# Long-convolution front of a gated block on one core: two channel halves staggered, one second-stage transform of kv per block, an order written as a table

## The chip, the cores and the metric

One core of a Trainium2 chip runs the whole program. The metric is the device time of one execution in microseconds (us). The kernel before has a median of 561.63 us over three runs (561.54, 561.63, 564.53). The profiled execution took 562.82 us, of which 561.0 us lie between its first and its last instruction (the span); its granted TensorE clock was 0.996 of full speed.

Engine names are those of the profile: PE (matrix multiply), PEld (its weight load), DVE (vector engine), ACT (scalar engine), POOL (GpSimd), SP (the engine that issues most DMAs). All engines take their instructions in the order of the program.

## The reference

S = 2048 rows, D = 448 channels, F = 1792. Cut to what matters:

```python
mod = (silu(c) @ w_mod).reshape(6, D)          # sa, ca, ga, sb, cb, gb
h = layernorm(q) * (1 + ca) + sa
kv = causal_conv4(k, shift_k) * v              # four taps per channel
y = irfft(rfft(pad(kv)) * rfft(pad(ssm_k)))[:S] + kv * ssm_D
x = q + ga * (h * y)                           # first half: the long convolution
h = layernorm(x) * (1 + cb) + sb
x = x + gb * ((sigmoid(h @ w_gate) * (h @ w_up)) @ w_down)
```

Everything is float32. The Fourier transforms are done as matrix products.

## The kernel before, in words

The program has two parts: the convolution (to about 158.8 us, where the first matmul `gu` of the gated unit starts) and the gated unit behind it, which is a long stream of matmuls. The change touches the first part and leaves the instructions of the second as they are, but for three small items named below.

The channels are cut into two halves of C = 224, h = 0 and 1. A transform of 4096 points is done in two stages. In stage one (`stage1`, L193) four matmuls of 64x128x224 go into a PSUM pair, and ACT evicts it into the tile `ak[h]` (kernel spectrum) or `av[h]` (kv); eight such groups fill one tile. (The profile has two records for each float32 matmul, so its counts are twice these.) Then DVE turns each of the 8 blocks of 896 columns (`turn`, L189, a 32x32 transpose). In stage two (`stage2_k`, L278) a block of `ak` is multiplied by `w2` on PE and evicted by ACT in place. For kv (`stage2_v`, L292) the same is done twice for each block: `w2[r, 0]` gives the real and imaginary parts, `w2[r, 1]`, which holds the same numbers rolled by 32, gives them swapped. So each block has 8 matmuls into two PSUM pairs, `pts[0]` and `pts[1]`. DVE multiplies each pair by the kernel's spectrum (L303, two products `m` of 128x896), PE adds up the products with `wa` (L319, tile `sa`, 4 matmuls) and DVE turns `sa` back into `av` (L321). Sixteen blocks (2 halves x 8) go through this loop, one block behind in `stage2_back`. Last, `stage_out` (L330) makes 16 rows of the output `y` out of all eight blocks of a half.

What feeds it: the four taps of the short convolution. `k` comes transposed in the tile `kT`, 112 partitions (a quarter of the channels, `ct`). There are 16 units, four quarters by four groups of rows. In 11 of them a first product is made by ACT (`conv_first`, L221) and three further taps are added by DVE (`conv_tap`, L226: one SCALAR_TENSOR_TENSOR of 112x512, out of `kT` and an accumulator, both in SBUF). In four units ACT makes all four products (L245), and one unit is done on PE with diagonal matrices (L260). PE transposes the sum into the PSUM pair `kv` (L263), and DVE multiplies `v` by it (`conv_mul`, L272).

Order: both halves of the kernel spectrum's stage one come first, then the short convolution of all channels together, then stage one of kv, and then the loop of 16 blocks. In that loop stand, beside the blocks: the remaining turns of `av` and `ak[1]`, stage two of `ak[1]`, the statistics of the layernorm of `q` (`ln1_stats`, L429, ACT), its gates (`gates`, L448; normalising on POOL for h = 0 and on ACT for h = 1, `modulate` L463 on POOL) and the six matrix products of `mod` (`mod_parts`, L369, `mod_sum`, L388). `mod` 3 and 5 come after the loop, between the outputs of the convolution and the first `gu`. The whole is recorded in a hand-written order; PSUM has eight banks in four pairs, two under the name `t`, and one each under `sa` and `y`.

All DMAs of the first part are issued by SP in program order, but two small ones by ACT.

Of the kernel before, what the change touches and what calls it, by code (L numbers as in the profile page):

```python
# [81 lines left out]
def adaln_conv_glu_kernel(ctx: ExitStack, tc: tile.TileContext, q, kT, v, ssm, shift, dskip,  # L82
# [26 lines left out]
    inb = big.tile([P, 16 * C], F32, tag="in", name="inb")  # L109
    taken = []  # L110

    def quad(tag, bufs, name):

        if tag == "in":
            at = len(taken) % 4 * 4 * C
            taken.append(name)
            return inb[:, at:at + 4 * C].rearrange("p (a c) -> p a c", c=C)
        return late["pg" if tag == "G" else "rb"].tile([P, 4, C], F32, tag=tag, bufs=bufs, name=name)

    def whole(t):  # L120
        return t.rearrange("p a c -> p (a c)").rearrange("p (g d) -> p g d", g=2)
# [8 lines left out]
    zc = pz.tile([P, NG, P], F32, name="zc")  # L130
    ktl = pk.tile([DT, 4, NG + 3, P], F32, name="kT")
    xin = {}
    early = big.tile([P, NG + 2, C], F32, tag="a0", name="early")
    ka, kb = slice(0, 11), (slice(11, 15), slice(15, NG + 3))

    def load_ssm(h, i, parts=(slice(0, 4),)):
        if (h, i) not in xin:
            xin[h, i] = early[:, 4 * i:4 * i + 4] if h else quad("in", 4, f"ssm{h}_{i}")
        t = xin[h, i]
        for s in parts:  # L140
            nc.sync.dma_start(t[:, s], ssm[:, h, 4 * i + s.start:4 * i + s.stop])
            if i == 0 and s.start == 0:
                dr = early[0:1, NG + h]
                nc.sync.dma_start(dr, dskip[:, h])
                (POOL if h else DVE).tensor_add(t[0:1, 0], t[0:1, 0], dr)

    def load_v(k):
        xin["v", k] = whole(quad("in", 4, f"v{k}") if k not in (4, 5) else spare[:, (k - 4) * 4 * C:(k - 3) * 4 * C].rearrange("p (a c) -> p a c", c=C))
        nc.sync.dma_start(xin["v", k], v[:, 2 * k:2 * k + 2])

    def load_k(ct, part):
        at = DT * ct * (NG + 3) * P
        w = (part.stop - part.start) * P
        at += DT * P * part.start
        nc.sync.dma_start(ktl[:, ct, part].rearrange("p a b -> p (a b)"), kT[at:at + DT * w].rearrange("(p x) -> p x", p=DT))
# [1194 lines left out]
```

## Time and profile before

| item | value |
| --- | --- |
| median of 3 runs | 561.63 us |
| profiled execution | 562.82 us |
| its span | 561.0 us |
| PE busy in the span | 544.9 us (97%) |
| DVE busy | 435.4 us (78%) |
| ACT busy | 271.9 us (48%) |
| POOL busy | 57.4 us (10%) |
| first turn of `ak[0]` on DVE | 16.04 us |
| first product `m` on DVE | 71.52 us |
| last turn of `sa` on DVE ends | 147.06 us |
| first `gu` on PE | 158.79 us |
| HBM read / written | 63.58 / 28.44 MB |

How to read it: the share of busy time is a mean over two parts with different limits. A row of a group names the line, the engine, the operation and the tiles (out<-in), the shape, how many there are, their busy time together, the mean of one in ns, and how long the engine had been idle in front of them and for whom. The chain is followed back from the last instruction to whatever released each step. A PE that counts as busy is not PE at its peak, since its ends are modelled.

### The profile page before, as it was taken

Reading aid. Unit: us, or ns where it says so; the run is one execution under the profiler, and the core shown is the slowest. Engines: PE = TensorE matmul, PEld = TensorE weight load, DVE = VectorE, ACT = ScalarE, POOL = GpSimd, SP = SyncE. Lnnn points to the kernel's source line nnn. Section 1 sums busy time; section 2 is a strip of 40 time slices with the busy share of each in tenths; the row PEclk is TensorE's granted clock in tenths of the full one; section 3 lists DMA queues with packets and bytes.
Section 4 is the critical chain, followed back from the end, with each engine's and each line's share of the span. In section 5 each row is a group of like instructions: output and inputs, shape, how many; then the busy total and the mean of one; then the engine's idle time right before and its main releaser. Section 6 shows DMA issues by size and latency. Waiting matters only on the chain.

```text
span 561.0 us, 7853 instructions
## 1 busy us (share of the span) xinstructions
PE 544.9 (97%) x3074; PEld 423.5 (75%) x3074; DVE 435.4 (78%) x544; ACT 271.9 (48%) x471; POOL 57.4 (10%) x52
## 2 busy tenths in 40 slices
PE   7898899999999999999999999999999999999997
PEld 6577632333567888888888888888888888888886
DVE  0879789969789887898998888885555556879565
ACT  4977676971477586366546462332122222334120
POOL 1000006979400000000000000000000000000000
PEclk9989999999999999999999999999999999999999
DMA  8993591200530408494968195676464662220103
GB/s 277 281 273 116 169 323 58 76 2 2 149 109 1 160 4 303 148 377 190 350 237 322 76 362 168 227 265 232 137 206 129 205 214 111 77 103 10 56 1 131
DMA packets 24857, 93.06 MB, mean 166 GB/s; under 512 B 3058, under 2 KB 4212, under 8 KB 23796
## 3 DMA queue, kind: packets, MB, share of 16 engines
q1 hardware_dynamic: 18372, 67.66, 38.0%
q10 hardware_dynamic: 6448, 24.90, 11.4%
q8 instruction: 24, 0.39, 0.3%
q14 instruction: 13, 0.11, 0.1%
HBM read 63.58 MB, written 28.44 MB: 164 GB/s over the span
## 4 chain that ended last, share of the span: by engine, by line
PE 76%; DVE 12%; DMA 4%; issue 3%; ACT 3%; SPq 1%; DVEq 0%; ACTq 0%
PE d L911 23%; PE b L877 16%; PE c L877 10%; PE a L877 10%; PE gu L1000 4%; PE s2v L300 3%; DVE m L303 3%; DMA kT<-in_kT_dram 2%; PE y L335 2%; PE sa L319 2%; PE s1v L199 2%; DVE av L321 2%; DMA early<-in_ssm_dram 1%; PE kv L260 1%; DVE av L191 1%
## 5 line engine op out<-in xcount | busy, mean ns | idle before, releaser
L911 PE MATMUL d<-wd,h 128*128 128x448 f32 x666 | 144.4, 366 | 0.6 <-DVE wd L497 0.5
L911 PEld LDWEIGHTS d<-wd,h 128*128 128x128 f32 x666 | 124.7, 188 | 13.5 <-DVE wd L497 1.4
L877 PE MATMUL b<-xt,ring 128*128 128x512 f32 x408 | 99.0, 391 | 0.0
L877 PEld LDWEIGHTS b<-xt,ring 128*128 128x128 f32 x408 | 76.5, 188 | 14.9 <-issue 0.2
L926 DVE TENSOR_TENSOR x<-x,d 128x896 f32<-128x896 f32 x55 | 59.5, 1084 | 16.6 <-PE d L911 16.6
L877 PE MATMUL a<-x,ring 128*128 128x512 f32 x264 | 63.8, 389 | 0.0
L877 PEld LDWEIGHTS a<-x,ring 128*128 128x128 f32 x264 | 49.6, 188 | 10.2
L886 ACT ACTIVATE h<-st 128x512 fp32r<-128x512 f32 x55 | 34.6, 629 | 31.4 <-DVE st L895 19.0
L889 DVE TENSOR_TENSOR h<-st,h 128x512 fp32r<-128x512 f32 x55 | 37.8, 688 | 12.5 <-ACT h L886 12.2
L892 ACT ACTIVATE st<-st 128x512 f32<-128x512 f32 x24 | 15.2, 631 | 63.6 <-DVE st L1237 35.8
L1000 PE MATMUL gu<-x,ring 128*128 128x512 f32 x176 | 42.5, 395 | 0.1
L1191 ACT ACTIVATE st<-st 128x512 f32<-128x512 f32 x12 | 7.6, 631 | 67.8 <-DVE st L1190 67.8
L303 DVE TENSOR_TENSOR m<-s2v,ak 128x896 f32<-128x896 f32 x32 | 33.2, 1078 | 9.2 <-PE s2v L300 8.2
L1000 PEld LDWEIGHTS gu<-x,ring 128*128 128x128 f32 x176 | 32.7, 188 | 7.7 <-ACT full L800 0.6
L877 PE MATMUL c<-x,ring 128*128 128x512 f32 x144 | 34.8, 390 | 0.0
L858 ACT ACTIVATE ring<-sum 128x512 fp32r<-128x512 f32 x28 | 17.3, 626 | 32.2 <-DVE sum L839 16.8
L877 PEld LDWEIGHTS c<-x,ring 128*128 128x128 f32 x144 | 27.0, 188 | 5.2
L300 PE MATMUL s2v<-av,w 64*64 64x448 f32 x256 | 30.8, 546 | 0.1
L877 PE MATMUL c<-xt,ring 128*128 128x512 f32 x120 | 29.2, 389 | 0.0
L319 PE MATMUL sa<-m,wa 128*64 128x448 f32 x128 | 27.4, 552 | 0.0
L877 PEld LDWEIGHTS c<-xt,ring 128*128 128x128 f32 x120 | 22.5, 188 | 4.6
L895 DVE TENSOR_TENSOR st<-st 128x512 f32<-128x512 f32 x24 | 16.6, 690 | 11.9 <-ACT st L892 11.7
(184 smaller groups left out, 787.9 us busy)
## 6 DMA issues: line engine op xcount, KB each, us to landing
fd<-ring ACTq DMA_DIRECT2D x35, 512.0 KB, 5.2
ring<-fd SPq DMA_DIRECT2D x35, 512.0 KB, 3.9
wdk<-wd ACTq DMA_DIRECT2D x7, 896.0 KB, 5.9
wd<-wdk SPq DMA_DIRECT2D x7, 896.0 KB, 4.8
inb<-in_wgu_dram SPq DMA_DIRECT2D x6, 1024.0 KB, 5.3
x<-in_q_dram SPq DMA_DIRECT2D x4, 896.0 KB, 8.5
wm<-in_wmod_dram SPq DMA_DIRECT2D x8, 392.0 KB, 5.5
out_dram<-x SPq DMA_DIRECT2D x7, 448.0 KB, 2.6
```

Source lines behind the costliest of these rows:

```text
L300: PE.matmul(pts[b][c:c + 64, ex, :D], w2[r:r + 64, ex], xs_[b][r:r + 64], start=True, stop=True)
L303: DVE.tensor_mul(m[b], rows(pts[b]), ks[b].unsqueeze(1).to_broadcast([P, 2, D]))
L319: PE.matmul(wide[r, b, :, :56], wa[:, b, r], m[b][:, ex], start=True, stop=True)
L858: ACT.activation(forms[name, i][:, 0], w_src(name), AF.Copy)
L877: PE.matmul(pt, wh(s, t), x[:, k], start=start and m == 0, stop=stop and m == len(ops) - 1, skip_group_check=True)
L886: ACT.activation(hh, h, AF.Copy)
L889: DVE.tensor_sub(hl, h, hh)
L892: ACT.activation(y[:, 0], y[:, 0], AF.Sigmoid)
L895: DVE.tensor_mul(y[:, 0], y[:, 0], y[:, 1])
L911: PE.matmul(y, h[:, (2 * e + i) * P:(2 * e + i + 1) * P], x, start=m == 0, stop=m == len(ops) - 1)
L926: DVE.tensor_add(y, y, rows(pt))
L1000: PE.matmul(pt[:, g], plain(q, t)[:, s, g, f * P:f * P + P], xf[xs_[b]][:, k], start=m == 0, stop=m == 10, skip_group_check=True)
```

## The change

- The order of the whole first part is a table of 436 items (`ORDER`), which `run` plays one by one: `t1.0.2.1.d.0` is tap 1 of half 0, rows 4i to 4i+3 with i = 2, quarter 1 of the half, on DVE, into accumulator 0; `p` is POOL, `a` ACT; `:0` to `:3` is the PSUM pair. The two halves follow each other, half 1 behind half 0.
- kv's stage two is done once for a block (`do_s2v`: 4 matmuls, one PSUM pair). DVE multiplies this pair twice: by the block of `ak` (`do_m0`) and by a copy of that block in which neighbouring groups of 32 partitions are swapped (`do_m1`). The copy is made by four DMAs of 32x896 from SBUF to SBUF (`do_kx`), in three homes in turn. `w2` loses its second half, and the right half of `wa` takes its rows in swapped order.
- The short convolution: the first product of all 16 units (`p`) is made by POOL, three taps of each unit of half 0 and two of half 1 by DVE, one product of each unit of half 1 by ACT. The diagonal matrices are gone. `k` is padded to 128 partitions and loaded in four parts a quarter; `v` and `w_mod` are cut and padded likewise.
- A new map of SBUF: the tiles of the first part are fixed places in a few large ones (`inb`, `av0`, `ak0`, `av1`, `spare`, `kTa`, `kTb`, `m`, `zc`).
- `mod` 3 and 5 move into the loop. `ln1_end`, in before half on ACT, is two DVE operations for each of its four groups.
- The four PSUM pairs have names of their own (`t0`, `t1`, `sa`, `y`).

```diff
+ORDER = """
+kt.0.0.0 kt.0.1.0 ssm.0.2 kt.0.1.1 kt.0.1.2 v.0.3 zc.3 kt.0.0.1 zc.2 kt.0.0.3 v.0.0 dr.1 dr.0 t0.0.0.1.p.0 ssm.0.0 kt.0.0.2 t0.0.0.0.p.1 t1.0.0.1.d.0
...
+"""
-    w2 = np.zeros((128, 2, 64))
+    w2 = np.zeros((128, 64))
...
+    wa[:, :, 64:] = wa[np.arange(128) ^ 32, :, 64:]
...
+    def do_kx(h, n, k):
+        to, of = kxs[k], block(ak[h], n)
+        for r in range(0, P, 32):
+            nc.sync.dma_start(to[r:r + 32], of[r ^ 32:(r ^ 32) + 32])
...
+    def product(h, i, c, tap, k, eng):
+        x = tap_in(h, i, c, tap)
+        a = x if k is None else accs[k]
+        terms.setdefault((h, i, c), {})[tap] = a
+        if eng is ACT:
+            ACT.activation(a, x, AF.Copy, scale=scale(h, c, tap))
+        else:
+            POOL.tensor_scalar(a, x, scale(h, c, tap), None, op0=OP.mult)
+
+    def add_tap(h, i, c, tap, n, eng):
+        x, t = tap_in(h, i, c, tap), terms[h, i, c]
+        a = x if tap == 3 else t[n]
+        eng.scalar_tensor_tensor(a, x, scale(h, c, tap), t[n], op0=OP.mult, op1=OP.add)
+        t[n] = a
...
+    def do_s2v(h, n, pt):
+        for b in range(2):
+            for r in (0, 64):
+                c = r ^ 64 * b
+                PE.matmul(pt[c:c + 64, b, :D], w2[r:r + 64], block(av[h], n)[r:r + 64, D * b:D * b + D], start=True, stop=True)
+
+    def do_m0(h, n, pt, k):
+        DVE.tensor_mul(pairs2(ms[:, k]), rows(pt), pairs2(block(ak[h], n)))
+
+    def do_m1(h, n, pt, k, kx):
+        DVE.tensor_mul(pairs2(ms[:, k]), rows(pt), pairs2(kxs[kx]))
...
-                for ex in range(2):
-                    for b in range(2):
-                        for r in (0, 64):
-                            c = r ^ 64 * b
-                            PE.matmul(pts[b][c:c + 64, ex, :D], w2[r:r + 64, ex], xs_[b][r:r + 64], start=True, stop=True)
-                m = [pairs(quad("m", 4, f"m{h}_{n}_{b}")) for b in range(2)]
-                for b in range(2):
-                    DVE.tensor_mul(m[b], rows(pts[b]), ks[b].unsqueeze(1).to_broadcast([P, 2, D]))
...
     def do_le(i):
         r, m = rstd[:, 4 * i:4 * i + 4], nmr[:, 4 * i:4 * i + 4]
         DVE.reciprocal(r, r)
-        if i in (0, 3):
-            DVE.tensor_mul(m, m, r)
-        else:
-            for k in range(4):
-                ACT.activation(m[:, k:k + 1], m[:, k:k + 1], AF.Copy, scale=r[:, k:k + 1])
+        DVE.tensor_mul(m, m, r)
...
-    mod_parts(3, "sa")
...
-    mod_parts(5, "y", gbrow, False)
...
-    mod_copy(5)
...
-        mod_sum(5)
```

Three places in the order show what moved. First DVE in the early part. In before, the first work of DVE behind its memsets and one small addition (L145) is the turning of `ak` (148 is half 0, 149 half 1), and taps (L229) follow:

```order
L145 TENSOR_TENSOR inb<-inb,early 1x224
L191 STREAM_TRANSPOSE ak_148<-ak_148 128x28x16x2 x8
L191 STREAM_TRANSPOSE ak_149<-ak_149 128x28x16x2 x4
L229 SCALAR_TENSOR_TENSOR acc_0_280<-kT,sk,acc_0_280 112x512
L229 SCALAR_TENSOR_TENSOR acc_1_288<-kT,sk,acc_1_288 112x512
```

In the change, DVE's first 26 taps (L302; `spare` and `m` hold the accumulators, `kTa` half 0 and `kTb` a quarter of half 1) stand ahead of the first turn of `ak` (L212); this is the end of that stretch, with two products of `v` and kv (L314, `av_83`):

```order
L302 SCALAR_TENSOR_TENSOR spare<-kTa,sk,spare 112x512 x5
L302 SCALAR_TENSOR_TENSOR kTa<-kTa,sk,spare 112x512 x2
L302 SCALAR_TENSOR_TENSOR spare<-kTb,sk,spare 112x512
L302 SCALAR_TENSOR_TENSOR kTb<-kTb,sk,m 112x512
L302 SCALAR_TENSOR_TENSOR spare<-kTa,sk,spare 112x512
L314 TENSOR_TENSOR av_83<-av_83,kv_2_0_272 128x896
L302 SCALAR_TENSOR_TENSOR kTa<-kTa,sk,spare 112x512
L212 STREAM_TRANSPOSE ak_81<-ak_81 128x28x16x2 x3
L314 TENSOR_TENSOR av_83<-av_83,kv_1_0_223 128x896
```

So turns and taps have changed places: what DVE begins with now needs `k`, not the kernel's spectrum.

Second POOL, from its first work on `mod` (L538, the copy to `scb`) to the first normalising of the gates (L459). Before:

```order
L537 TENSOR_TENSOR arow<-ident,sk 112x112 x4
L538 COPY scb<-cols 112x128
L145 TENSOR_TENSOR early<-early 1x224
L459 TENSOR_SCALAR G_0_823<-x_626,rstd,nmr 128x224 x4
L465 TENSOR_TENSOR G_0_823<-G_0_823,arow 128x896
```

In the change (L550 is the copy, L297 the products of tap 0, L226 the addition of the skip term, L459 the gates in the old place of `kTa`):

```order
L550 COPY scb<-cols 112x128
L297 TENSOR_SCALAR spare<-kTa,sk 112x512 x5
L226 TENSOR_TENSOR inb<-inb,gbrow 1x224
L297 TENSOR_SCALAR spare<-kTa,sk 112x512 x3
L297 TENSOR_SCALAR spare<-kTb,sk 112x512 x2
L297 TENSOR_SCALAR spare<-m,sk 112x512
L226 TENSOR_TENSOR av_83<-av_83,gbrow 1x224
L297 TENSOR_SCALAR m<-m,sk 112x512 x2
L297 TENSOR_SCALAR spare<-m,sk 112x512
L297 TENSOR_SCALAR spare<-kTb,sk 112x512 x2
L459 TENSOR_SCALAR kTa<-x_88,rstd,nmr 128x224 x8
```

Sixteen products have come to an engine that had four small ones, and they fall into the time of DVE's taps.

Third PE in the loop. Before, one block (the third of half 0: `s2v` is stage two of kv, `sa` the sum of the block ahead of it):

```order
L300 MATMUL s2v_2_0_759<-av_402,w_79 64x448 x2
L300 MATMUL s2v_2_1_760<-av_402,w_79 64x448 x2
L300 MATMUL s2v_2_0_759<-av_402,w_79 64x448 x2
L300 MATMUL s2v_2_1_760<-av_402,w_79 64x448 x2
L319 MATMUL sa_1_773<-m_1_0_741,wa 64x8x56 x2
L319 MATMUL sa_1_773<-m_1_1_742,wa 64x8x56 x2
```

In the change, two blocks and a half of the same place (L329 `s2v`, L342 `sa`, L277 stage two of `ak`):

```order
L329 MATMUL s2v_1_693<-av_79,w_89 64x448 x4
L342 MATMUL sa_0_703<-m,wa 64x8x56 x4
L329 MATMUL s2v_2_715<-av_79,w_89 64x448 x4
L277 MATMUL s2k_4_725<-ak_82,w_89 64x448 x4
L277 MATMUL s2k_2_731<-ak_82,w_89 64x448 x4
L342 MATMUL sa_1_741<-m,wa 64x8x56 x4
L342 MATMUL sa_2_750<-m,wa 64x8x56 x4
```

A block's `s2v` is half as long, and stage two of `ak` of half 1 has come into the first blocks of the loop.

More of the change, by code (lines that the diff above doesn't have):

```diff
@@ L107, in pairs, with flat @@
         return x.rearrange("p (b j) c -> p b (j c)", b=2)
[L109 to L121, printed above, removed]
+    def flat(t, at, n, parts=P):
+        return t[:parts, at:at + n]
     def small(shape, name, src=None):
@@ L127, in small @@
         return t
[L130 to L155, printed above, removed]
@@ L161, in adaln_conv_glu_kernel @@
+    pairs2 = lambda t: t.rearrange("p (b c) -> p b c", b=2)
+    gt = {(h, i): quarter(g_home[h][i]) for h in range(2) for i in range(4)}
+    KP = slice(0, 7), slice(7, 11), slice(11, 15), slice(15, NG + 3)
+    w2 = small([P, 64], "w2")
     sk = small([DT, 4, 4], "sk")
@@ L265, in conv_mul @@
-    def conv_mul(i, unit=None):
-        for e in range(2):
-            if unit:
-                conv_tap(*unit, 2 * e + 1)
-                if e == 0:
-                    pass
-            x = xin["v", 2 * i + e]
-            DVE.tensor_mul(x, x, rows(kvs[i, e]))
-            if unit and not e:
-                conv_tap(*unit, 2)
-    def half(a, n, b):
-        return block(a, n)[:, D * b:D * b + D]
-    def stage2_k(h, n, tag):
-        pt = two(tag, f"s2k{h}_{n}")
+        ACT.activation(d, y, AF.Copy)
@@ L281, in stage2_k, with do_s1k, do_e1k, do_tk @@
+    def do_s1k(h, i, e, pt):
+        stage1(h, 4 * i + 2 * e, quarter(block(ssm_t[h], i))[:, 2 * e:2 * e + 2], pt)
+    def do_e1k(h, i, e, pt):
+        evict1(ak[h], h, 4 * i + 2 * e, pt)
+    def do_tk(h, n):
+        turn(ak[h], n)
+    def do_s2k(h, n, pt):
         for b in range(2):
-            x = half(ak[h], n, b)
             for r in (0, 64):
                 c = r ^ 64 * b
-                PE.matmul(pt[c:c + 64, b, :D], w2[r:r + 64, 0], x[r:r + 64], start=True, stop=True)
-        ACT.activation(block(ak[h], n).rearrange("p (b c) -> p b c", b=2), rows(pt), AF.Copy)
@@ L310, in stage2_back, with do_ek, tap_in, scale @@
-    def stage2_back(between=None):
-        h, n, m = products.pop(0)
-        pt = two("t" if h and n == 7 else "sa", f"sa{h}_{n}")
+                PE.matmul(pt[c:c + 64, b, :D], w2[r:r + 64], block(ak[h], n)[r:r + 64, D * b:D * b + D], start=True, stop=True)
+    def do_ek(h, n, pt):
+        ACT.activation(pairs2(block(ak[h], n)), rows(pt), AF.Copy)
+    terms = {}
+    def tap_in(h, i, c, tap):
+        return ktl[2 * h + c][:DT, 4 * i + 3 - tap:4 * i + 7 - tap]
+    def scale(h, c, tap):
+        return sk[:, 2 * h + c, tap:tap + 1]
@@ new lines, in do_kv, with do_vm, do_s1v @@
+    def do_kv(h, i, c, pt):
+        ts = list(terms[h, i, c].values())
+        for g in range(4):
+            y = pt[:, g // 2, g % 2 * C + c * DT:g % 2 * C + c * DT + DT]
+            for k, a in enumerate(ts):
+                PE.matmul(y, a[:, g], ident[:DT, :DT], start=k == 0, stop=k == len(ts) - 1, is_transpose=True)
+    def do_vm(h, i, pt):
+        x = pairs2(block(v_t[h], i))
+        DVE.tensor_mul(x, x, rows(pt))
+    def do_s1v(h, i, e, pt):
+        stage1(h, 4 * i + 2 * e, quarter(block(v_t[h], i))[:, 2 * e:2 * e + 2], pt)
@@ L369, in adaln_conv_glu_kernel, with open_tmp, do_y, do_yc @@
-    mods = {}
-    def mod_parts(m, tag, part=None, copy=True):
-        pr = two(tag, f"mod{m}") if type(tag) is str else tag
-        for h in range(2):
-            wm = wms.pop((m, h))
+    def open_tmp():
+        t = late["tmp"] = big.tile([P, 32 * C], F32, tag="k0", name="tmp")
+        ring["raw"] = t[:, NG * C:NG * C + 6 * 512].rearrange("p (t g f) -> p t g f", t=6, g=2)
+    def do_y(h, i, pt):
+        stage_out(h, i, None, pt=pt)
+    def do_yc(i, pt):
+        y_copy(0, i, rows(pt))
@@ L714, in first_forms @@
         plain_hi(0, 2)
[L716 to L718 removed]
+    first_forms()
     for t in (0, 1, 3):
```

534 lines of the change are left out of this document (209 added, 325 removed).

## The prediction

> **What bounds the kernel now.** I read the stages first, then the chain, then the groups. The chain says where the change can work at all: up to the first `gu` at 158.8 us. The table of stages (us, busy by engine with records, TensorE clock, DMA share, GB/s) cuts this part at DVE's first turn, first product and last turn.
>
> ```profile
> core 0: us, PE busy (x) PEld busy (x) DVE busy (x) ACT busy (x) POOL busy (x), PEclk, DMA share, GB/s
> 0.00:16.00 16.00, 13.00 (x98) 11.75 (x100) 1.21 (x7) 8.39 (x11) 3.09 (x13) 1.00 0.85 292
> 16.00:71.50 55.50, 49.04 (x435) 36.58 (x431) 45.59 (x56) 43.48 (x60) 0.00 (x0) 0.97 0.75 204
> 71.50:147.10 75.60, 73.25 (x556) 26.05 (x558) 68.68 (x74) 46.07 (x112) 51.08 (x37) 1.00 0.27 90
> 147.10:158.80 11.70, 11.51 (x139) 7.96 (x135) 8.33 (x19) 8.27 (x18) 3.25 (x2) 1.00 0.46 120
> 158.80:561.00 402.20, 398.15 (x1856) 341.20 (x1856) 311.56 (x389) 165.72 (x274) 0.00 (x0) 1.00 0.49 171
> ```
>
> Behind 158.8 us PE is busy 398.15 of 402.2 us with work that the change leaves alone: a microsecond won ahead of `gu` is won at the end. In front of it DVE is the engine to watch: 115.5 us busy (1.21 + 45.59 + 68.68) in 147.1, so idle 14.8 us before 16, 9.9 in the short convolution, 6.9 in the loop of blocks. The chain shows the loop changing hands:
>
> ```profile
> 102.03 1.07 DVE m L303
> 103.11 1.02 DVE av L321
> ...
> 130.36 1.65 PE sa L319 x8
> 132.01 0.79 PE y L335 x8
> 132.80 1.66 PE s2v L300 x16
> 134.47 1.65 PE sa L319 x8
> ```
>
> A block there takes 4.1 us (130.36 to 134.47), PE without a gap; earlier in the loop the same block waits for DVE. So a saving on PE alone is worth little unless DVE also has less to wait for. The groups carry the prices (busy us, mean ns, then idle before them and for whom):
>
> ```profile
> L303 DVE TENSOR_TENSOR m<-s2v,ak 128x896 f32<-128x896 f32 x32 | 33.2, 1078 | 9.2 <-PE s2v L300 8.2 <-issue 1.0
> L300 PE MATMUL s2v<-av,w 64*64 64x448 f32 x256 | 30.8, 546 | 0.1
> L319 PE MATMUL sa<-m,wa 128*64 128x448 f32 x128 | 27.4, 552 | 0.0
> L321 DVE STREAM_TRANSPOSE av<-sa 128x896 f32<-128x896 f32 x16 | 17.7, 1105 | 0.1
> L191 DVE STREAM_TRANSPOSE av<-av 128x896 f32<-128x896 f32 x16 | 17.2, 1078 | 0.8 <-ACT av L206 0.8
> L191 DVE STREAM_TRANSPOSE ak<-ak 128x896 f32<-128x896 f32 x16 | 16.3, 1072 | 9.1 <-ACT ak L206 9.1
> L229 DVE SCALAR_TENSOR_TENSOR acc<-kT,sk,acc 112x512 f32<-112x512 f32 x22 | 15.5, 744 | 4.7 <-ACT acc L224 4.7
> L285 PE MATMUL s2k<-ak,w 64*64 64x448 f32 x128 | 15.0, 557 | 3.3 <-ACT ak L286 1.3 <-DVE av L321 1.1 <-DVE brow L395 1.0
> L272 DVE TENSOR_TENSOR inb<-inb,kv 128x896 f32<-128x896 f32 x6 | 6.2, 1082 | 1.5 <-PE kv L263 1.5
> L335 PE MATMUL y<-av,wb 128*64 128x224 f32 x96 | 11.2, 363 | 0.0
> ```
>
> **DVE's work.** Products, turns and evictions of `sa` stay as they are: 32, 32 and 16 operations. Taps go from 33 to 40: 7 x 0.705 (15.5 / 22) = +4.9 us. Small items (an eviction and an addition leave, two small multiplications come) give -1.2. DVE then needs 115.5 + 3.7 = 119.2 us ahead of the last turn. Up to the first product stand 1.2 of memsets, 40 taps (28.2), 8 `kv` products (8.3), 16 turns of `ak` and 7 of `av` (23 x 1.05 = 24.1): 61.8. Behind it stand 57.4.
>
> **The start.** The first tap needs two chunks of `k` (2 x 448 KB) and one POOL product. A small DMA landed 2.7 us after issue, and the first stage moved 292 GB/s:
>
> ```profile
> sk<-in_shift_dram ACTq DMA_DIRECT2D x1, 7.0 KB, 2.7
> ...
> L459 POOL TENSOR_SCALAR G<-x,rstd,nmr 128x224 f32<-128x224 f32 x16 | 8.2, 528 | 76.1 <-PE s2v L300 73.3 <-issue 2.7
> ...
> L466 POOL TENSOR_TENSOR G<-G,brow 128x896 f32<-128x896 f32 x4 | 8.4, 2101 | 0.3
> ```
>
> Data at 0.7 + 2.7 + 0.92 MB / 292 GB/s = 6.5 us. A straight line through POOL's 528 ns for 224 columns and 2101 for 896 gives 1.2 us for 512, so the first tap runs at 7.7 us: DVE idles 6.5 us where it idled 14.8.
>
> **The early part.** DVE was busy 45.59 of 55.5 us. Of its idle time, 4.7 us were taps waiting for ACT's first products, which now come from POOL. Without them the share is 45.59 / 50.8 = 90%; I take that for the 60.6 us behind the start: 67.3 us, first product at 75.0. Loads hide under this as long as they keep pace. Two stretches of the queue, 8 to 16 us (`ssm`, 128 partitions) and 16 to 26 us (mostly `kT`, 112 partitions), ran at
>
> ```profile
> DMA packets 1189, 3.27 MB, mean 409 GB/s; under 512 B 136, under 2 KB 200, under 8 KB 1189
> ...
> DMA packets 634, 2.69 MB, mean 269 GB/s; under 512 B 72, under 2 KB 137, under 8 KB 633
> ```
>
> so padding `k` to 128 may pay. The `v` of half 1 that DVE wants at about 60 us stands behind some 16 MB in SP's order (counted in the table): there at 42 us by the faster rate, at 62 by the slower, which would cost DVE 2 to 5 us. PE loses the diagonal matmuls and ACT 19 products net there, both off DVE's path: nothing.
>
> **POOL beside the taps.** In before no tap runs beside POOL: all lie in the stage from 16 to 71.5 us, where POOL has 0.00 (x0). The two small operations with two SBUF tensors on DVE later in the loop also fall between POOL's:
>
> ```profile
> 87.87 0.16 DVE L442 TENSOR_TENSOR nmr<-nmr,rstd 128x4 f32<-128x4 f32 x1
> ...
> 122.94 0.16 DVE L442 TENSOR_TENSOR nmr<-nmr,rstd 128x4 f32<-128x4 f32 x1
> ```
>
> ```profile
> 88.30 2.06 POOL L459 TENSOR_SCALAR G<-x,rstd,nmr 128x224 f32<-128x224 f32 x4 [73.34 <-PE s2v L300]
> ...
> 123.27 2.06 POOL L459 TENSOR_SCALAR G<-x,rstd,nmr 128x224 f32<-128x224 f32 x4 [2.75 <-issue]
> ```
>
> So the price of a product meeting a tap is unknown. From below it is nothing: turns (one SBUF tensor) have means of 1072 ns (`ak`, most with POOL at rest) and 1078 (`av`, most beside it). From above it is the whole product, 1.2 us, with DVE standing; a gain I exclude, as a wait can't shorten a tap. Some 11 of the 16 products are due while DVE has only taps (an accumulator is refilled once its third tap is done); the rest meet turns. That is 0 to 13.2 us. I take half, 6.6, since a tap that comes at some moment of a running product waits half of it on average: first product of `m` at 81.6. The Trainium skill ("SBUF — State Buffer", section "Who interferes with whom") says that a DVE instruction with two SBUF inputs and a POOL instruction that reads SBUF lock each other out for the whole instruction. No row here tests it; by it the sum would hold the upper end, 13.2.
>
> **The loop.** PE's sum there: 16 `s2v` now at the price of `s2k` (15.0 / 16 = 0.94), 16 `sa` at 1.71, 8 `s2k` at 0.94, three `y` at 1.87, and 7 for `mod` (0.90 a product, 0.76 and more a sum, rows below): 62.5 us, where before it was 73.25. DVE has 57.4, or 63.2 at its old share of 90.8%. Both say 63, 12.4 less than the 75.6 of before; 9 turns (9.4 us) of that have only moved ahead of the loop, with 7 taps. So the halved `s2v` gives PE 16 us and the end little, because DVE is next. The last turn ends at 81.6 + 63.2 = 144.8, where it was 147.1: 2.3 us.
>
> **The tail.** From the last turn to `gu` PE led:
>
> ```profile
> 150.13 0.90 PE mod L377 x16
> 151.02 1.74 PE y L335 x16
> 152.76 0.76 PE mod L402 x6
> 153.85 0.89 PE mod L377 x16
> 154.74 1.74 PE y L335 x16
> ...
> 158.73 0.43 ACT gbrow L386
> ```
>
> `mod` 3 and 5 leave: 0.90 + 0.76 + 0.89 = 2.55 on PE, and twice some 0.5 on ACT behind it. Against that, `y` 3 and the sums of `mod` 5 now stand ahead of `y1_0` (about 1.3), and next in line is DVE's chain of additions and statistics. I take 1.5 us gained, between 0 and 2.5.
>
> **Sum.** 562.8 - 2.3 - 1.5 = 559.0 for the profiled execution, which lies 1.2 us above the median of the runs: 557.8, say 558.
>
> **Rivals.** (1) The products cost nothing and the order leaves DVE hardly idle. For it: half 1's work stands ready whenever half 0 waits, which before it did not. At 95% the early part ends at 7.7 + 63.8 = 71.5, the loop at PE's 62.5, the last turn at 134.0: 13.1 + 1.5 gained, 548 us as a median (544 to 552).
>
> (2) Slower: every product stops the taps for its whole length. Place: DVE between 8 and 40 us; price 13.2 instead of 6.6, then about 2 for the small multiplications of L442's kind, now four and beside POOL's 2.1 us operations, and 2.3 in the tail, where DVE adds `x1` and `inb` while POOL finishes the gates. That is +10.9 on 558 = 569; what it fills of DVE's idle 10% early (6.7 us) comes off: 562. So 562 to 569, 566 in the middle. It decides from about 8 products paid in full. For it: the two rows of L442 above, which avoid POOL, so that nothing contradicts it; against: turns beside POOL lose nothing. This is what the rule of the Trainium skill named above makes of the time.
>
> (3) The swapped copies come late. Nearest row, 128 KB from SBUF to SBUF on 64 partitions (ns of an issue; landing in us):
>
> ```profile
> L803 SPq DMA_DIRECT2D full<-full x4: 467/564/700, 189.9 to 334.7; - x4
> ...
> DMA to landing us min/median/max: 4.6/6.0/7.7
> ```
>
> Four issues and a landing are 4 x 0.56 + 6.0 = 8.2 us (6.5 to 10.5). A home is free for three blocks less a product, 3 x 3.95 - 1.0 = 10.8, so it fits by 2.6 us. But SP waits in order: loads of `mod`'s weights and of the gated unit stand between the copies, each pair of 448 KB ahead of a copy adds 2.2 us at 409 GB/s, and `m1` holds the turns behind it on DVE. 12 us would cost 1.2 for each three blocks, 6.4 in all: 564.
>
> **Chances.** Forecast 0.38 (553 to 562), rival 1 0.24, rival 2 0.26, rival 3 0.12. A measurement of this kernel tells about 0.5%, 2.8 us, from no change. Below 558.8: 0.22 + 0.24 + 0.01 = 0.47. Within: 0.14 + 0.07 + 0.05 = 0.26. Above 564.4: 0.02 + 0.19 + 0.06 = 0.27. The range 545 to 568 takes in most of rivals 1 and 2; cases of both signs hold it, and the forecast's own is 553 to 562.
>
> **What would show it.** Right: DVE's first tap near 7.7 us, first `m` near 81.6, last turn near 144.8, `gu` near 155. Taps that last or wait longer where POOL has a product decide between 1 and 2: 0.7 us each and a first turn of `ak` near 28 us is rival 1, a first turn near 38 us rival 2. `m` waiting for a DMA into `kTb` is rival 3. The forecast is wrong in its ground if DVE's idle time in the loop goes to PE's `s2v` again, or if the time moves behind the first `gu`.

## The result and the profile after

The changed kernel takes 553.33 us (median of four runs, 553.13 to 553.48) where the kernel before took 562.13 in the runs beside it: a ratio of 0.9835, 95% interval 0.9805 to 0.9865. Its profiled execution has a span of 551.3 us against 561.0. So 9.7 us were gained (8.8 by the medians), where 3.8 had been forecast. Of the four executions of the kernel with the halves kept apart, shown further down, the profiled one took 1064.9 us and the others about 568, so that kernel was run once more.

The table of stages of the kernel after, cut at the same landmarks (DVE's first tap, first product `m`, end of the last turn, first `gu`):

```profile
core 0: us, PE busy (x) PEld busy (x) DVE busy (x) ACT busy (x) POOL busy (x), PEclk, DMA share, GB/s
0.00:8.15 8.15, 4.64 (x20) 4.34 (x20) 0.83 (x7) 1.49 (x2) 2.77 (x10) 1.00 0.78 274
8.15:72.98 64.83, 55.32 (x468) 39.77 (x468) 62.46 (x71) 46.90 (x69) 27.65 (x17) 0.95 0.77 282
72.98:135.15 62.17, 58.88 (x464) 22.11 (x462) 61.43 (x68) 37.20 (x86) 47.88 (x35) 1.00 0.71 197
135.15:149.50 14.35, 9.67 (x90) 6.76 (x83) 9.82 (x19) 8.72 (x17) 6.23 (x3) 0.94 0.01 2
149.50:551.30 401.80, 398.18 (x1856) 341.61 (x1854) 311.34 (x389) 164.80 (x272) 0.00 (x0) 1.00 0.49 171
```

| landmark, us | before | forecast | after |
| --- | --- | --- | --- |
| first tap | (16.0, a turn) | 7.7 | 8.15 |
| first product `m` | 71.5 | 81.6 | 72.98 |
| last turn ends | 147.06 | 144.8 | 135.15 |
| first `gu` | 158.79 | near 155 | 149.50 |

DVE is busy 123.9 of the 127.0 us between its first tap and its last turn. The loop has become 13.4 us shorter (75.6 to 62.17) although the first `m` is 1.5 us later. From the last turn to the first `gu` 2.65 us were lost again (11.7 to 14.35). Behind `gu` nothing changed (402.2 and 401.8).

All of DVE's waits in the early part, from the chain of waits of the kernel after (total, times, longest):

```profile
DVE spare L302 <- DMA kTa<-in_kT_dram: 6.2, 1, 6.2
DVE spare L302 <- POOL spare L297: 1.1, 3, 0.4
DVE m L302 <- POOL m L297: 0.4, 1, 0.4
DVE inb L314 <- PE kv L310: 0.4, 1, 0.4
DVE m L302 <- ACT spare L295: 0.2, 1, 0.2
```

The first row is the start. Behind it only 2.1 us remain. The taps have grown, most of all those that run beside POOL's products. These are the two largest of their eight groups, which sum to 32.4 us for 40 taps; the forecast's price for a tap without a neighbour gave 28.2:

```profile
L302 DVE SCALAR_TENSOR_TENSOR spare<-kTa,sk,spare 112x512 f32<-112x512 f32 x16 | 14.3, 929 | 7.4 <-DMA kTa<-in_kT_dram 6.2 <-POOL spare L297 1.1
L302 DVE SCALAR_TENSOR_TENSOR kTa<-kTa,sk,spare 112x512 f32<-112x512 f32 x8 | 6.3, 812 | 0.1
```

The swapped copies land early, and the products that read them wait for nothing (the row of the copies among the DMA issues, with the median time to landing; the group of `m` in the loop):

```profile
kTb<-ak SPq DMA_DIRECT2D x64, 112.0 KB, 3.0
```

```profile
L335 DVE TENSOR_TENSOR m<-s2v,kTb 128x896 f32<-128x896 f32 x16 | 17.2, 1076 | 0.1
```

The tail, from the timeline of the kernel after (start, duration):

```profile
135.20 2.08 POOL L464 TENSOR_TENSOR zc<-zc,brow 128x896 f32<-128x896 f32 x1
...
137.14 2.04 PE L361 MATMUL y<-av,spare 128*64 128x196 f32 x32
...
137.36 4.15 POOL L397 TENSOR_TENSOR tmp<-tmp,zc 128x896 f32<-128x896 f32 x2
...
138.87 1.15 DVE L618 TENSOR_TENSOR inb<-inb,y 128x784 f32<-128x784 f32 x2 [3.72 <-PE y L361]
...
139.93 2.60 DVE L621 TENSOR_TENSOR x<-x,inb 128x784 f32<-128x784 f32 x2
```

DVE waits 3.72 us for the first output of half 1, since `mod` 5 stands ahead of it on PE (`y1_0` below is this first output). Then its additions L621 take 2.60 us instead of the 1.15 of before. They end 1.02 us behind POOL's last gate (137.36 + 4.15 = 141.51).

### The profile page after: what moved, and what is told of

Its sections match the earlier page's. It is cut to its first block, busy times and chain, and to the rows that moved or that the text cites. A ratio compares the mean times of both kernels' runs of the same rounds, so it can differ in the third digit from the quotient of the medians.

```text
span 551.3 us, 7602 instructions
## 1 busy us (share of the span) xinstructions
PE 526.7 (96%) x2886; PEld 414.6 (75%) x2886; DVE 445.9 (81%) x551; ACT 259.1 (47%) x444; POOL 84.5 (15%) x64
## 4 chain that ended last, share of the span: by engine, by line
PE 75%; DVE 10%; ACT 5%; DMA 4%; issue 3%; SPq 2%; POOL 0%; DVEq 0%; ACTq 0%
PE d L793 24%; PE b L759 16%; PE c L759 10%; PE a L759 10%; PE gu L881 5%; PE s1k L257 2%; DMA kTa<-in_wmod_dram 2%; SPq L249 1%; PE sa L342 1%; PE kv L310 1%; PE y L361 1%; PE s1v L257 1%; DVE spare L302 1%; PE s2k L277 1%; ACT gbrow L441 1%
## 5 line engine op out<-in xcount | busy, mean ns | idle before, releaser
L881 PEld LDWEIGHTS gu<-x,ring 128*128 128x128 f32 x176 | 33.4, 192 | 7.0 <-DVE inb L922 0.3
L342 PE MATMUL sa<-m,wa 128*64 128x448 f32 x128 | 27.1, 548 | 2.4 <-DVE m L335 2.4
L777 DVE TENSOR_TENSOR st<-st 128x512 f32<-128x512 f32 x24 | 16.6, 691 | 11.9 <-ACT st L774 11.7
L342 PEld LDWEIGHTS sa<-m,wa 128*64 128x64 f32 x128 | 8.4, 136 | 20.1 <-issue 12.1
L262 ACT ACTIVATE ak<-s1k 128x896 f32<-128x896 f32 x16 | 14.4, 920 | 19.0 <-PE s1k L257 19.0
```

The lines of the kernel that those rows point to most:

```text
L262: ACT.activation(d, y, AF.Copy)
L342: PE.matmul(wide[r, b, :, :56], wa[:, b, r], pairs2(ms[:, k])[:, b], start=True, stop=True)
L777: DVE.tensor_mul(y[:, 0], y[:, 0], y[:, 1])
L881: PE.matmul(pt[:, g], plain(q, t)[:, s, g, f * P:f * P + P], xf[xs_[b]][:, k], start=m == 0, stop=m == 10, skip_group_check=True)
```

## The experiments

Theory A: the staggered order leaves DVE no idle, and the halved stage two keeps PE from becoming the bound, so both are needed. Its rivals: the padded loads did it (B); or DVE's waits went because ACT and PE lost work, whatever the order (C). For the tail: `mod` 5 on PE costs it (T1), or POOL's gates do, through DVE's additions (T2). All ratios are against the kernel before, run beside each. Their intervals are 0.2 to 0.6% wide on each side, so where kernels differ by less, the landmarks in the traces carry the reading. Line numbers move by one to three in kernels with added lines.

**Stage two of kv at its old price.**

```diff
+                for _ in range(2):
-                PE.matmul(pt[c:c + 64, b, :D], w2[r:r + 64], ...)
+                    PE.matmul(pt[c:c + 64, b, :D], w2[r:r + 64], ...)
```

> The changed kernel with each matmul of kv's stage two issued twice into the same PSUM pair with the same operands (the output stays the same): PE gets its old 16 x 0.94 = 15.0 us back, DVE and the swapped copies stay. Theory A (with this order DVE is busy without a break, and PE has only 62.2 - 58.9 = 3.3 us to spare in the loop): the loop becomes PE's, 58.9 + 15.0 = 73.9 us instead of 62.2, last turn at 147, time 564 to 566 us, so that without the halved stage two nothing of the gain is left. Rival (DVE's order is what the gain comes from, and PE's saving lies beside it, as the forecast had it: of 16 us on PE the end gets little): +3 to 5 us, 556 to 558.

Measured: 561.09 us, ratio 0.9982 (0.9962 to 1.0003). The whole gain is gone. The loop in this kernel:

```profile
73.10:144.10 71.00, 70.32 (x584) 28.14 (x584) 61.36 (x67) 37.21 (x86) 51.49 (x37) 1.00 0.63 173
```

PE is busy 70.32 of 71.00 us: it is the bound. The second issue cost PE 11.4 us, not 15, so the loop grew by 8.8 us; 1.65 came back in the tail, where POOL was done earlier. So in this order, without the halved stage two, everything else in the change together is worth nothing measurable.

**The halves' early work kept apart.** The table is reordered up to the first `m`; nothing else changes. One row of it, from which half 1's items are gone (they follow behind half 0's last):

```diff
-kv.0.3.1 s2k.0.0:3 tk.0.3 e1v.0.2.1 wm.1 s2k.0.2:0 vm.0.1 ek.0.0 s1k.1.3.1:3 vm.0.3 ek.0.2 s1v.0.1.1:2 t2.1.1.0.d.0 e1k.1.3.1 da.1 s1v.0.3.0:1 tk.0.4
+s2k.0.2:0 vm.0.1 ek.0.0 vm.0.3 ek.0.2 s1v.0.1.1:1 s1v.0.3.0:3 tk.0.4 e1v.0.1.1 s1v.0.1.0:2 e1v.0.3.0 s1v.0.3.1:0 e1v.0.1.0 tk.0.1 s2k.0.4:1 e1v.0.3.1
```

> The changed kernel with the table reordered up to the first product m: all early work of half 0 first (taps, stage one of spectrum and kv, turns), then that of half 1, each in its old order; loads of k, the spectrum, v of half 0 stay in front; PSUM pairs are dealt anew. Nothing is added or left out. Theory A (the other half's work fills DVE's waits, which is why only 2.4 us of idle were left between 8.15 and 72.98 us): DVE's idle there goes back to the 10% that it had before, 6 to 8 us, first m near 78, time 557 to 560 us. Rival C (DVE's waits went because ACT and PE lost work and POOL makes the products; the order has no part in it): first m within 1 us of 73, time 553 to 554.

Measured: 568.23 us, ratio 1.0107 (1.0067 to 1.0147). Both theories had the size wrong. The kernel ran once more for its profile:

> The kernel with the halves apart once more, for its profile: its time was 568.2 us, 15 above the changed kernel, more than theory A (557 to 560) had. Theory A2: the other half's work fills DVE's waits, and for PE and ACT too: DVE stands behind stage one of kv of half 0 and again behind that of half 1, 12 us or more of idle between the first tap and the first m in two or three long pieces. Rival: DVE's idle is 6 to 8 us as A had it, and the rest is lost in the loop, where turns of av of half 1 and the second stage of ak came later.

Measured: 571.57 us, one run. The stage from the first tap to the first `m` there:

```profile
8.11:92.02 83.91, 59.64 (x467) 41.40 (x467) 62.66 (x71) 48.29 (x69) 27.72 (x17) 0.86 0.59 215
```

DVE has 62.66 us of work, as in the changed kernel (62.46), and 21.3 us of idle instead of 2.4. The loop behind it is as long as there (62.3 us). So C falls, and the size is that of A2. The places are A2's only in part: DVE waits 1.8 us for stage one of kv of half 0, and the longest piece, 9.3 us ahead of the first `m`, begins when half 1 is nearly done, as the next experiment shows.

**Only the taps apart.** As above, but stage one of half 1's spectrum stays between the work of half 0. Against the row above:

```diff
-s2k.0.2:0 vm.0.1 ek.0.0 vm.0.3 ek.0.2 s1v.0.1.1:1 s1v.0.3.0:3 tk.0.4 e1v.0.1.1 s1v.0.1.0:2 e1v.0.3.0 s1v.0.3.1:0 e1v.0.1.0 tk.0.1 s2k.0.4:1 e1v.0.3.1
+s2k.0.2:0 vm.0.1 ek.0.0 s1k.1.3.1:1 vm.0.3 ek.0.2 s1v.0.1.1:3 e1k.1.3.1 da.1 s1v.0.3.0:2 tk.0.4 e1v.0.1.1 s1v.0.1.0:0 e1v.0.3.0 s1v.0.3.1:1 e1v.0.1.0
```

> The kernel with the halves apart, but stage one of half 1's spectrum (PE and ACT) back between the work of half 0, so that only half 1's taps, its products with v and stage one of its kv follow half 0's early work. Theory A (DVE's waits come from the order of the taps themselves): most of the 21.3 us of idle that the halves apart had between first tap and first m stay, 12 to 18 us, time 562 to 566. Rival (they came from stage one of the spectrum of half 1, which stood between half 1's taps on PE and ACT): idle 3 to 6 us, time 554 to 557.

Measured: 570.33 us, ratio 1.0145 (1.0107 to 1.0183), more than either theory had. The stage again has 81.89 - 62.24 = 19.7 us of idle, and DVE's two longest waits in it are

```profile
DVE spare L302 <- POOL spare L297: 9.3, 5, 6.5
DVE m L332 <- PE s2v L329: 8.5, 1, 8.5
```

The first includes 6.5 us of the start. What stands behind the second is seen in the other engines:

```profile
79.87 1.73 ACT L262 ACTIVATE av<-s1v 128x896 f32<-128x896 f32 x2 [0.19 <-PE s1v L257]
...
82.38 0.57 ACT L440 ACTIVATE gbrow<-x 128x448 f32<-128x448 f32 x1
...
85.80 1.33 PE L417 MATMUL part<-kTa,ones 128*128 128x448 f32 x2 [3.41 <-ACT kTa L412]
...
88.71 1.49 PE L329 MATMUL s2v<-av,w 64*64 64x448 f32 x8
```

Half 1's last eviction ends at 81.6. Then ACT makes statistics of the layernorm (L440), the sum of `mod` 1 on PE (L417) waits for an ACT copy behind them, and `mod` 0 follows; the first `s2v` stands behind all this in PE's order. In the changed kernel the same items lie between the work of half 1. In both tables that keep the halves apart they come behind it, so that the first `m` is 8.7 us behind the last eviction here and 9.5 in the other table, where it is 2.0 in the changed kernel. Some 7 of the 20 us of idle are thus not owed to the halves; the 13 that are left, an estimate, still lie far above 2.4.

**The phases of the kernel before.** Spectrum of both halves first, then all taps, then stage one of kv. The row in which the first phase ends and the taps begin:

```diff
+e1k.1.3.0 e1k.1.1.1 s1k.1.2.0:3 e1k.1.2.0 tk.0.0 tk.0.2 tk.0.3 tk.0.4 tk.0.1 tk.0.5 tk.0.6 tk.0.7 t0.0.0.1.p.0 t0.0.0.0.p.1 t1.0.0.1.d.0 t2.0.0.1.d.0
```

> The changed kernel with the table reordered up to the first product m into the phases of the kernel before: loads of both halves of the spectrum first, stage one of both halves, the eight turns of ak 0, then the short convolution of half 0 and of half 1, then stage one of kv, then the rest. Nothing is added or left out. Theory A: DVE starts with turns at about 15 us instead of with a tap at 8.15 (7 us), and waits again for about 10% of its time behind that (4 to 6 us more): first m 84 to 86, time 564 to 567 us. Rival C (the order matters only through what DVE starts with): the start alone, first m near 80, time 560 us.

Measured: 587.02 us, ratio 1.0444 (1.04 to 1.0489). DVE's longest waits there (the first row is the start):

```profile
DVE ak L212 <- ACT ak L262: 18.9, 1, 18.9
DVE m L332 <- PE s2v L329: 6.8, 1, 6.8
DVE av L212 <- ACT av L262: 6.6, 1, 6.6
DVE inb L314 <- PE kv L310: 4.5, 3, 1.9
```

The same work idles 20 us ahead of its first turn and 24.9 behind it (86.49 - 61.61). These three tables are plain sorts, not tuned orders, and all three also move the statistics and `mod` 1 and 0 behind half 1's stage one of kv. PE's granted clock was lower in them too (0.86, 0.83 and 0.70 in this stage against 0.95), and with the halves and the taps apart PE was busy 4.3 and 6.0 us longer there; how much of DVE's idle comes from that, no run separates. They show that the order sets DVE's idle ahead of the first `m`, from 9.7 us to 44.9 with the same instructions, and that the halved stage two in a poor order is slower than the kernel before. They don't show how well a tuned order without the stagger could do.

**k unpadded.**

```diff
-nc.sync.dma_start(ktl[ct][:, s]..., kT[at:at + P * w].rearrange("(p x) -> p x", p=P))
+nc.sync.dma_start(ktl[ct][:DT, s]..., kT[at:at + DT * w].rearrange("(p x) -> p x", p=DT))
```

> The changed kernel with k loaded unpadded on 112 partitions (in the same four parts a quarter). Rival B (the loads were what DVE waited for, and the padding is what took the idle time away): 4.36 MB at 269 instead of about 400 GB/s are 5.3 us more of transfer ahead of v and of half 1, DVE stands 4 to 5 us more before the first m, time 557 to 559 us. Theory A (order, not rate): the first tap about 0.5 us later, the rest hidden, first m 73.3 to 74.5, time 553.5 to 555.

Measured: 553.6 us, ratio 0.9853 (0.9815 to 0.9892), the time of the changed kernel. The early stage:

```profile
8.10:72.80 64.70, 55.02 (x468) 39.50 (x468) 62.32 (x71) 46.80 (x69) 27.67 (x17) 0.95 0.83 278
```

It is the same stage, at 278 GB/s against 282. Where the loads are densest (16 to 26 us) the queue moved 353 GB/s against 393, but no wait of DVE grew by it. B falls, and with it the remark that padding may pay.

**Products of tap 0 by ACT**, all 16 as this one.

```diff
-t0.0.0.1.p.0
+t0.0.0.1.a.0
```

> The changed kernel with the first product of all 16 units made by ACT instead of POOL, at the same place of the table. Theory A (POOL's products cost the taps 32.4 - 28.2 = 4.2 us and 1.5 us of waits, no more): taps fall from a mean of 810 to about 705 ns (4.2 us), but ACT, 46.9 us busy in the 64.8 us ahead of the first m, gets 16 x 0.6 = 9.6 us and its evictions come later, so DVE waits for ACT as it did in before (4.7 us): net 552 to 556. Rival (the products on POOL cost the taps their whole length, 16 x 1.75 = 28 us less what DVE would have idled): first m 8 us or more earlier, time 547 or less.

Measured: 552.62 us, ratio 0.9816 (0.9759 to 0.9874). The first tap comes at 6.44 us, the first `m` at 71.55, and the 40 taps take 29.3 us instead of 32.4; this is the largest group:

```profile
L302 DVE SCALAR_TENSOR_TENSOR spare<-kTa,sk,spare 112x512 f32<-112x512 f32 x16 | 11.4, 748 | 4.9 <-ACT spare L295 4.8
```

So POOL's products cost the taps 3.1 us and the start 1.7. In exchange DVE's idle behind the first tap rises from 2.37 to 5.72 us (65.11 - 59.39), mostly for ACT. Of the 1.4 us won at the first `m`, 0.7 is left at the end.

**The disputed price by itself.** Stretches of DVE's and POOL's operations, alone and beside each other.

> A kernel by itself that leaves the whole computation out and only runs stretches of operations of this kernel's kinds, on DVE and POOL alone and beside each other, with a meeting point between the stretches: 24 taps (two SBUF tensors) and 10 products of 512 columns; 16 turns (one SBUF tensor) and 10 products; 16 products m (PSUM and SBUF) and 10 products; then taps, turns, m and additions of two SBUF tensors beside 8 gates (POOL, 128x896, two SBUF tensors); last 24 taps beside 12 POOL memsets, which read nothing. Theory L (a DVE operation with two SBUF tensors and a POOL operation that reads SBUF never run at the same time, whichever comes first is waited for): taps beside products take as long as both apart, 24 x 0.71 + 10 x 1.55 = 32.5 us, additions beside gates 16 x 1.0 + 8 x 2.1 = 33 us; turns, m, and taps beside memsets lose nothing. Rival S (they share, as the 4.2 us that 16 products cost the 40 taps could be read): taps beside products stretch by some 15%, to about 20 us, products by 15%.

Alone (busy us, mean ns), from the groups of the first stretches:

```profile
L152 DVE SCALAR_TENSOR_TENSOR acc<-kt,sk,acc 112x512 f32<-112x512 f32 x24 | 17.4, 750 | 0.6
L156 POOL TENSOR_SCALAR prod<-kt,sk 112x512 f32<-112x512 f32 x8 | 12.3, 1563 | 0.1
L177 POOL TENSOR_TENSOR ga<-ga,gb 128x896 f32<-128x896 f32 x6 | 12.2, 2068 | 0.0
L173 DVE TENSOR_TENSOR da<-da,db 128x896 f32<-128x896 f32 x12 | 12.1, 1084 | 0.0
```

Taps beside products:

```profile
L152 DVE SCALAR_TENSOR_TENSOR acc<-kt,sk,acc 112x512 f32<-112x512 f32 x24 | 21.0, 899 | 0.6
L156 POOL TENSOR_SCALAR prod<-kt,sk 112x512 f32<-112x512 f32 x10 | 18.1, 1830 | 0.0
```

Taps beside gates:

```profile
L152 DVE SCALAR_TENSOR_TENSOR acc<-kt,sk,acc 112x512 f32<-112x512 f32 x24 | 31.3, 1328 | 0.6
L177 POOL TENSOR_TENSOR ga<-ga,gb 128x896 f32<-128x896 f32 x8 | 19.4, 2457 | 0.0
```

Additions of two SBUF tensors beside gates, from the row of their line (least, median and longest ns):

```profile
L173 DVE TENSOR_TENSOR da<-da,db x28: 1077/1080/17277, 62.7 to 236.4; 128x896 f32<-128x896 f32 x28
```

Beside POOL's products the rival S holds: 10 products of 1.54 us and 24 taps of 0.75 would need 33.4 us in turn and took 21.6 from first to last; a product costs the taps 0.36 us. Beside POOL's gates theory L holds: one tap goes between two gates (2.4 to 2.6 us each while they last), and one addition stood for 17.28 us, about the length of all eight gates and its own. Turns beside either took 1.00 us each, as alone, products `m` 1.00, and taps beside memsets 0.75.

**The tail: `mod` 5 behind y1_0.**

```diff
-... y.0.3:2 gm.0.2 st.1.7 st.1.6 part.5:3 yc.3 pc.5 sum.5 ga.2 sc.5 ga.3
+... y.0.3:2 gm.0.2 st.1.7 st.1.6 yc.3 ga.2 ga.3
     y10.append(stage_out(1, 0, "t", parts[1]))
+    run("part.5:3 pc.5 sum.5 sc.5")
```

> The changed kernel with the product and the sum of mod 5 (and their two ACT copies) issued behind y1_0 instead of ahead of it. Theory T1 (that sum, which waits for ACT, holds y1_0 for 2.0 us, and DVE behind it for 3.72): y1_0 starts at 135.2 instead of 137.14, the first gu 2.0 us earlier, time 551.3. Rival T2 (DVE's additions of x1 and inb wait for POOL's gates in any case: 2.60 us beside L397 that took 1.15 in before): the additions end only when POOL's operation ends, 0 to 1 us gained, time 552.3 to 553.3.

Measured: 553.37 us, ratio 0.9835 (0.9795 to 0.9875): nothing gained. Its timeline shows why:

```profile
137.10 1.15 DVE L619 TENSOR_TENSOR inb<-inb,y 128x784 f32<-128x784 f32 x2 [1.78 <-PE y L361]
...
137.54 4.87 POOL L397 TENSOR_TENSOR tmp<-tmp,zc 128x896 f32<-128x896 f32 x2
138.17 4.38 DVE L622 TENSOR_TENSOR x<-x,inb 128x784 f32<-128x784 f32 x2
```

DVE starts 1.8 us earlier, and the additions then take 4.38 us and end where they did (142.55, after 142.53). T1's wait was real and worth nothing, because POOL's gates came next.

**The gates held back.** A tiny POOL copy that reads `nmr` stands ahead of both L397.

```diff
-... st.1.6 part.5:3 yc.3 pc.5 sum.5 ga.2 sc.5 ga.3
+... st.1.6 part.5:3 yc.3 pc.5 sum.5 sc.5
...
+    POOL.tensor_copy(cols[:, 23:24], nmr2[:, 0:1])
+    run("ga.2 ga.3")
```

> The changed kernel with POOL's last two gates (L397, tmp times zc) held back until DVE has made the second statistics of the first four rows (one tiny POOL copy that reads nmr stands ahead of them). Theory T2 (the additions of x1 and inb take 2.60 instead of 1.15 us because a DVE operation with two SBUF tensors waits for POOL's operation to end): they take 1.15 again, first gu 1.4 us earlier, time 551.9. Rival (the additions wait for something else, PE's second part of y1_0 for example, or DVE's subtractions L533 then meet the gates instead): within 0.5 us of 553.3.

Measured: 556.4 us, ratio 0.9887 (0.9847 to 0.9928), 3 us slower. The additions took 1.16 us, as T2 said. But the gates then met the normalising of `xn`, which takes 1.36 us in the changed kernel:

```profile
144.26 4.90 DVE L659 TENSOR_SCALAR xn<-x,rstd,nmr 128x448 f32<-128x448 f32 x3
...
144.66 4.25 POOL L397 TENSOR_TENSOR tmp<-tmp,zc 128x896 f32<-128x896 f32 x2 [0.25 <-ACT tmp L369]
```

**The small multiplication of the statistics on ACT.**

```diff
-        DVE.tensor_mul(m, m, r)
+        for k in range(4):
+            ACT.activation(m[:, k:k + 1], m[:, k:k + 1], AF.Copy, scale=r[:, k:k + 1])
```

> The changed kernel with the small multiplication of two SBUF tensors in the statistics (L450, four of 128x4 on DVE: 0.16, 0.16, 1.11 and 0.82 us) made on ACT in 16 small operations of 0.2 us. Theory A (two of them stood until POOL's 2.1 us operation ended, and DVE has no idle to hide that in): DVE's loop loses 1.6 to 2.3 us, time 551.2 to 552. Rival (PE, 58.9 of 62.2 us in the loop, or ACT's later evictions take it up): within 0.5 us of 553.3.

Measured: 552.61 us, ratio 0.9831 (0.9789 to 0.9874). The last turn ends 1.6 us earlier (133.6), as expected, but the additions stand 3.09 us beside the gates, and the first `gu` comes only 0.5 us earlier.

**POOL relieved.** `mod` 5 behind y1_0 as above, and two normalisings moved to ACT.

```diff
-            if h:
+            if h or i > 1:
                 ACT.activation(gt[h, i][:, k], x1[:, g, cs], AF.Identity, bias=..., scale=...)
```

> The changed kernel with two edits: mod 5 behind y1_0 as in the tail experiment, and the normalising of the gates of half 0, groups 2 and 3 (two times four operations of 128x224, 2.05 us each time on POOL), made by ACT. POOL is busy without a gap from 89.9 to 141.5 us, so it ends 4.1 us earlier. Theory T2 (DVE's additions waited for POOL's gates L397 to end, and that took the gain of the tail experiment away): the additions take 1.15 us, y1_0 starts at 135.4, they end near 139.3 instead of 142.5, time 550.1. Rival T3 (y1_0 or the additions are not what the first gu waits for, and the stretch behind it takes up what is won): 552.5 to 553.5.

Measured: 550.54 us, ratio 0.981 (0.9785 to 0.9834). The first `gu` comes at 147.0, 2.5 us earlier. The additions still took 2.94 us, not 1.15: the gates also began earlier (135.00) and ran beside them.

**The last gate behind the additions**, on top of that.

```diff
-... st.1.6 yc.3 ga.2 ga.3
+... st.1.6 yc.3 ga.2
...
+    POOL.tensor_copy(cols[:, 23:24], x1[:, 3, D - 1:D])
+    run("ga.3")
```

> The kernel of the last tail experiment (mod 5 behind y1_0, normalising of groups 2 and 3 on ACT), and POOL's last gate (one of the two L397) held back behind DVE's additions of x1 and inb, by one tiny POOL copy that reads x1. There the additions still took 2.94 us, since the first gate began at 135.0 and ended at 137.1, and the second came at once. Theory T2 (each addition of two SBUF tensors waits for the POOL gate that runs): with POOL idle they take 1.15 us, end near 138.4 instead of 140.2, time 548.7. Rival (the held gate then meets DVE's normalising xn, which waits in its turn, as it did with the late gates): 550 to 551.

Measured: 549.83 us, ratio 0.9787 (0.9757 to 0.9817).

```profile
135.14 2.12 POOL L397 TENSOR_TENSOR tmp<-tmp,zc 128x896 f32<-128x896 f32 x1
136.32 1.15 DVE L619 TENSOR_TENSOR inb<-inb,y 128x784 f32<-128x784 f32 x2 [1.78 <-PE y L361]
137.38 1.15 DVE L622 TENSOR_TENSOR x<-x,inb 128x784 f32<-128x784 f32 x2
...
138.74 2.10 POOL L397 TENSOR_TENSOR tmp<-tmp,zc 128x896 f32<-128x896 f32 x1
```

The additions have their 1.15 us back, and the first `gu` comes at 145.8. The stretch from last turn to `gu` is 11.3 us, 0.4 below that of the kernel before. T2 holds.

**The first two products by ACT**, the others by POOL, on top of that.

```diff
-t0.0.0.1.p.0 ssm.0.0 kt.0.0.2 t0.0.0.0.p.1
+t0.0.0.1.a.0 ssm.0.0 kt.0.0.2 t0.0.0.0.a.1
```

> The kernel with the gate behind the additions, and the first two products of tap 0 made by ACT, the other 14 by POOL. Theory A (DVE has no idle behind its first tap, so an earlier start is won in full): first tap near 6.5 instead of 8.15 us, time 1.3 to 1.7 below the kernel without it: 547.2. Rival (the next waits, for v or for kv, take it up, as half of it was with all products on ACT): 548 to 548.7.

Measured: 547.51 us, ratio 0.9742 (0.9714 to 0.977), the fastest kernel here. The first tap comes at 6.68 instead of 7.99 us, the last turn at 132.1 and the first `gu` at 143.4, each 2.4 us earlier than without it. What is won at DVE's start arrives at the end. That it is more than the 1.3 us of the start was not followed up; the first taps, no longer beside a product, take 2.20 us instead of 3.05.

**All in one.** Products and the small multiplication on ACT, with the tail of the relieved POOL: the diffs of those three experiments together.

> All that the experiments point to in one kernel: the changed kernel with products of tap 0 on ACT, the small multiplication of the statistics on ACT, mod 5 behind y1_0, and the normalising of groups 2 and 3 on ACT. If the parts add up: 553.3 - 0.7 - 0.7 - 3.2 = 548.7 us. Rival (PE, busy 58.9 of 62.2 us in the loop, or ACT, which gets some 17 us more work, takes its place): 550 to 552.

Measured: 552.61 us, ratio 0.9834 (0.9807 to 0.9861). The parts did not add up. (The 3.2 was the forecast for the relieved POOL, whose time was not known yet; it gained 2.8.) DVE waited 2.2 us for ACT's square roots (L445) in the loop, and the additions stood 3.88 us beside the gates.

## Why the prediction was wrong, point by point

The direction was right, the size not: 9.7 us instead of 3.8. The step that failed is the early part, "Without them the share is 45.59 / 50.8 = 90%; I take that for the 60.6 us behind the start". Against the forecast the early part up to the first `m` came out 8.6 us better, the loop 1.0, the stretch behind `gu` 0.4, and the tail 4.15 worse: 5.9 us in all.

- **The start.** 8.15 us against 7.7: a product takes 1.54 us alone and not the 1.2 of the straight line, which ran through two other kinds of operation.
- **The early part, the failed step.** It was to last 60.6 of work, 6.7 of idle and 6.6 for POOL; it lasted 64.83. Idle behind the first tap was 2.37 us, 1.5 of it for POOL's products, so 0.9 stands against 6.7. The 10% belonged to the order of before, and I carried it over as if it belonged to the work. The tables that keep the halves apart show what it depends on: 20 to 21 us of idle with the same instructions (some 7 of them from the statistics and `mod` 1 and 0). Another 2.3 us came from counting with the means of groups. Neighbouring operations overlap in the records: the groups of this stage sum to 65.5 us, the busy time is 62.46.
- **POOL beside the taps.** 4.2 us of longer taps (3.1 by the kernel with the products on ACT, where 40 taps took 29.3 and not 28.2) and 1.5 of waits: 4.6 to 5.7 against the 6.6 taken. That the size is near is luck, since its reason (a tap waits half of a running product) was not so. A product costs the taps 0.36 us, and of the two kinds tried only the gates stop them. The rule of the Trainium skill ("SBUF — State Buffer", section "Who interferes with whom"), by which both engines lock each other out for the whole instruction, fits the gates and does not fit the products: the measurement decides, and for this operation it says sharing.
- **The loop.** 62.17 against 63.2, but by two misses that cancel. DVE's idle was 0.7 us and not the 5.8 of its old share, so the failed step was taken here a second time. And its work was 61.43 and not 57.4: the 2.3 us that the early part had too many were missing here, and the four small multiplications L450 took 2.3 us, 1.6 more than at 0.16 each. PE's sum, 62.5, measured 58.88. So PE and DVE are nearly level there. "So the halved `s2v` gives PE 16 us and the end little" was misleading: taken away, it costs the whole gain, 7.8 us. That little was reckoned from a first `m` 10 us behind that of before; it came 1.5 behind.
- **The tail.** Forecast 1.5 gained, measured 2.65 lost. Taking `mod` out of this stretch was half done (`mod` 5 stayed ahead of `y1_0`; what stood there was priced at 1.3 us and held it 2.0), and POOL's gates now run beside DVE's additions (1.45 us more, 2.60 - 1.15). The second was priced at 2.3 us, but in rival 2 and not in the forecast.
- **Rivals.** Rival 1 (order without idle) came nearest: first `m` 71.5 and last turn 134.0 forecast, 72.98 and 135.15 measured. Its ground held for the idle and not for the products, which cost 4.6 to 5.7 us, so that it came near is in part luck. By the forecast's own reckoning its median would be 547, since the 1.2 us between profiled execution and median were not taken off. The tail, which rival 1 had as a gain, kept the time at 553.3 rather than 548. Rival 2 fell: the first turn of `ak` came at 33.4 us, halfway between its mark and rival 1's, and products are not paid in full; its price for the small multiplications (2 us, measured 1.6) was near. Rival 3 fell: the copies landed in 3.0 us, half of what the nearest row gave, and no `m` waited for them.

## What to carry to other kernels

An engine's idle share belongs to an order of the work and not to the work: when an order is replaced, count the engine's work, ask for each wait what else now stands ready, and take the floor as a case of its own with a good chance. A saving on one engine is worth what the next engine leaves: the new order without the halved stage two was worth nothing here, and with it 8 us. Where VectorE and GpSimd both work out of SBUF, look at which of their operations meet: moving one GpSimd gate behind VectorE's additions brought the second pair of them from 2.94 us to 1.15, and moving two gates to a place where they met another VectorE operation cost 3 us.
